# Linear-attention and gated-FFN kernel on one core: a third place for scores and P, other places for the 64-row blocks' k and v, and weight pairs that lie 1.5 pieces ahead of their words

## Chip, cores and metric

One core of one Trainium2 chip runs the whole program. The metric is the device time of one execution in microseconds: 651.5 us before the change, the median of three runs (650.5 to 652.1).

## What is computed

Attention with a memory over 4 batches, 8 heads, 576 tokens and 64 features per head, and then a gated FFN with an RMS norm over the 2304 tokens (model width 512, inner width 1536). Cut to what matters:

```python
scores = (q @ k.T) / sqrt(64);  scores[causal] = -1e9
a = exp(scores - max);  a = a / (a.sum(-1) + 1e-9);  local = a @ v
qp = where(q > 0, q + 1, exp(q))
mem = (qp @ M_prev) / (qp @ z_prev + 1e-6)
x = sigmoid(beta) * mem + (1 - sigmoid(beta)) * local
xn = x / sqrt(mean(x*x) + 1e-6) * rms_g
g = xn @ w_gate
out = (g * sigmoid(g) * (xn @ w_val)) @ w_out
```

w_gate, w_val, w_out and rms_g arrive as 64-bit words.

## The kernel before

**Tiling.** The tokens are cut into 18 blocks of 128 rows. Of each pair of batches eight blocks are full blocks of one batch, and the ninth holds the last 64 rows of both (the 64-row blocks are 8 and 17, and `is_tail` names them). Two blocks make one chunk of the FFN, so there are nine chunks of 256 tokens. The FFN of a chunk takes 12 tiles F of the inner width (`m_proj`: gate and val into PSUM tile gv), and the product with w_out (`m_down`: PSUM tiles out0 and out1).

**Attention of a block** goes in units, each a group of four heads or fewer: `u_scores` (scores on PE, L515, and masked into the SBUF tile S by DVE, L521, with the maximum nm), `u_exp` (exp on ACT in place, L567, and a cast of its f16 part into P16, L572), `u_lo` (the remainder S - P16 into the second half of P16, on DVE or POOL, L581, and then one DMA transpose of P16 into PT, L583), and `u_pv` (PV on PE, L605 to L607). In the names of the trace P16 is P. S and P16 take the pool's two places each. `mem` (L642) is phi(q) times the memory, from the transposed tile phT. When a block's t is summed, ACT takes its square sum xs (L244) and casts it to x (L95), and a DMA transpose gives xT, which a chunk's first product (L872) needs. Blocks 0 and 1 and chunk 0 are computed in f32 (L865, L919), everything later in f16 with three terms per product (L872; L927 to L929).

**Weights.** There are 24 pieces of w_gate and w_val in three thirds (eight pieces a third: two matrices, four slices of the model width), and 12 pieces of w_out. They are loaded as 64-bit words, turned to f32 (`f64_to_f32`, L781 to L783), and after a scale for the third is known (rgs, wos) split into a pair of f16 halves, in place: the pair p lies one slot ahead of its words, so that the hi half of p covers the first half of the words of p - 1, and the lo half the second. `split` has two ways:

```python
if way == "0":
    hi_cast(dst_hi, src, scale)          # ACT L95
    lo_cast(dst_lo, src, scale, dst_hi)  # DVE L98
...
nc.vector.tensor_scalar(src, src, scale, None, op0=ALU.mult)  # way 3: L112
nc.scalar.copy(dst_hi, src)                                   # L114
nc.gpsimd.tensor_tensor(dst_lo, src, dst_hi, ALU.subtract)    # L117
```

`SPLIT` is the table of ways by third; its third entry "033" sends five of the last third's eight pieces by way 3.

**Places.** `load_kv` brings a block's k and v into one of four places of the tag kv (4 KB per partition), or, for a 64-row block, into the one place of the tag kvt. The tag kT has ten places of 2 KB, the tag res has one place of 4 KB, through which the outputs leave (L905) and some words of w_out come (rawo).

**Order.** SyncE issues nearly all DMAs from one queue in program order. The order on each engine is set when the program is built: a list of attention steps with costs, and `run`, `zipped` and `proj` near L1175 to L1200, which lay weight splits and FFN tiles between them; a scheduler then moves instructions by priority and by when a place is free.

Of the kernel before, what the change touches and what calls it, by code (L numbers as in the profile page):

```python
# [9 lines left out]
F32 = mybir.dt.float32  # L10
# [32 lines left out]
SPLIT = ("0", "0", "033", "0")  # L43
# [15 lines left out]
def attn_memory_moe_kernel(  # L59
# [112 lines left out]
    wgv = const.tile([P, 2 * NC * NT3 + 1, 512], F32, name="wgv")  # L172
    wo = const.tile([P, NF + 1, 512], F32, name="wo")
    wgv16 = wgv.bitcast(F16)
    wo16 = wo.bitcast(F16)
# [28 lines left out]
    zs = const.tile([P, 4], F32, name="zs")  # L204

    def load_kv(n):
        tag = "kvt" if is_tail[n] else "kv"
        stage[n] = sb.tile([P, 2, HD], F32, tag=tag, name=f"kv{n}", bufs=1 if is_tail[n] else 4)
        if n >= 2:
            nc.sync.dma_start(out=stage[n], in_=qkv[n, :, :2, :])  # L210

    def load_half(n, j):
        nc.sync.dma_start(out=stage[n][:, j], in_=qkv[n, :, j, :])
# [37 lines left out]
    def stat_blk(b, i):  # L251
        if b < 2:
            r = slice(0, P) if i < NI else slice(b * TR, b * TR + TR)
            src = pre.pop((b, i), None)
            if src is None:
                kv = stage[blk_of[(b, i)] if i < NI else NI * 2]
                src = [kv[r, j] for j in range(2)]
            for j in range(2):
                if i == 0:
                    csum["kv", b, j] = ps.tile([P, 512], F32, tag="out", name=f"csum{j}")  # L260
                gram(csum["kv", b, j], src[j], i == 0, i == NI)
                if i == NI:
                    nc.vector.tensor_reduce(
                        stt[b][:, j, 0:1], csum.pop(("kv", b, j))[:, :P], axis=AX.X, op=ALU.max
                    )
            return
        if i < NI:
            for j in range(2):
                square_acc(stage[blk_of[(b, i)]][:, j], stt[b][:, j, i : i + 1])
        else:  # L270
            n = blk_of[(b - b % 2, NI)]
            r0 = (b % 2) * TR
            for j in range(2):
                square_acc(stage[n][r0 : r0 + TR, j], stt[b][r0 : r0 + TR, j, NI : NI + 1])
# [119 lines left out]
    def prep_qk32(n):  # L394
        k32[n] = sb.tile([P, NC, P], F32, tag="kT", name=f"k32_{n}", bufs=10)
        last["k", n] = transposed(k32[n], stage[n][:, 0], T32[0] == "a")
        q32[n] = sb.tile([P, 2, NC, P], F32, tag="qT", name=f"q32_{n}")
        last["q", n] = transposed(q32[n][:, 0], qst[n], T32[1] == "a")
# [163 lines left out]
    def u_exp(n, h0):  # L562
# [5 lines left out]
        p16 = sb.tile([P, 2 * (NI * P + P)], F16, tag="P16", name="P16")  # L568
# [442 lines left out]
    def lead_steps(n):  # L1011
# [18 lines left out]
        if n == NI * 2 - 1:  # L1030
            st[6].append((0.0, lambda: load_kv(blk_of[(nb, NI)])))
# [186 lines left out]
    run(zipped([lambda d=d: (m_down(d), wo_split(d)) for d in range(NF)], spl(2)), goal)  # L1218
# [79 lines left out]
```

## Time and profile before

| | before |
|---|---|
| runs | 651.5 us median, 650.5 to 652.1, three runs |
| profiled execution, its own time | 652.67 us |
| its span in the trace | 651.0 us |
| mean granted TensorE clock | 0.964 |
| PE (TensorE matmul) busy | 606.2 us, 93% |
| DVE busy | 468.1 us, 72% |
| ACT busy | 383.2 us, 59% |
| POOL busy | 172.7 us, 27% |

A timeline row gives an instruction's start and length, its engine, line, operation, what it writes and reads, the shape, and in brackets how long the engine was idle before it and what ended that. Positions in us count from the start of the span. PE matmuls overlap in the pipeline, so the length of one matmul row is longer than the distance to the next; a row with x20 is a run of twenty.

### The profile page before, as it was taken

Reading aid. Unit: us, or ns where it says so; the run is one execution under the profiler, and the core shown is the slowest. Engines: PE = TensorE matmul, PEld = TensorE weight load, DVE = VectorE, ACT = ScalarE, POOL = GpSimd, SP = SyncE. Lnnn points to the kernel's source line nnn. Section 1 sums busy time; section 2 is a strip of 40 time slices with the busy share of each in tenths; the row PEclk is TensorE's granted clock in tenths of the full one; section 3 lists DMA queues with packets and bytes.
Section 4 is the critical chain, followed back from the end, with each engine's and each line's share of the span. In section 5 each row is a group of like instructions: output and inputs, shape, how many; then the busy total and the mean of one; then the engine's idle time right before and its main releaser. Section 6 shows DMA issues by size and latency. Waiting matters only on the chain.

```text
span 651.0 us, 16007 instructions
## 1 busy us (share of the span) xinstructions
PE 606.2 (93%) x6131; PEld 472.7 (73%) x6131; DVE 468.1 (72%) x1444; ACT 383.2 (59%) x803; POOL 172.7 (27%) x257
## 2 busy tenths in 40 slices
PE   6899997898999599898999999999999999999996
PEld 4788785456766388687787777777878788888774
DVE  4689997788989765796877857968887757862221
ACT  4446776477688756575567666756665545532222
POOL 4020331112463333231242312422232212112211
PEclk9689998798999889999999999999999999999999
DMA  8977999539437997546859773595657464440001
GB/s 255 406 257 281 265 284 193 84 54 231 81 81 157 169 185 136 83 88 130 166 113 176 138 121 74 95 159 110 132 119 115 91 84 87 86 75 18 32 1 33
DMA packets 188524, 88.63 MB, mean 136 GB/s; under 512 B 173568, under 2 KB 173600, under 8 KB 188448
## 3 DMA queue, kind: packets, MB, share of 16 engines
q1 hardware_dynamic: 187680, 85.49, 61.0%
q0 software_dynamic: 768, 2.12, 1.0%
q8 instruction: 48, 0.79, 0.5%
q14 instruction: 28, 0.23, 0.1%
HBM read 36.20 MB, written 4.72 MB: 63 GB/s over the span
## 4 chain that ended last, share of the span: by engine, by line
PE 38%; DVE 7%; ACT 5%; DMA 5%; issue 3%; SPq 0%; POOL 0%; ACTq 0%
PE gv L872 20%; PE out L927 3%; PE out L928 3%; PE out L929 3%; PE sc L541 2%; DVE P L581 2%; PE sc L515 1%; DMA PT<-P 1%; DMA kT<-row 1%; ACT junk L244 1%; DMA xT<-x 1%; DVE S L521 1%; ACT S L567 1%; DVE th L883 1%; DMA kv<-in_qkv_dram 1%
## 5 line engine op out<-in xcount | busy, mean ns | idle before, releaser
L872 PE MATMUL gv<-xT,wgv 128*128 128x256 f16 x2304 | 314.0, 275 | 3.5 <-DMA xT<-x 3.5
L872 PEld LDWEIGHTS <-wgv 128*128 128x128 f16 x2304 | 221.9, 98 | 40.3 <-issue 4.4
L898 POOL TENSOR_TENSOR h<-th,h 128x256 f16<-128x256 f32 x96 | 71.5, 745 | 262.7 <-ACT h L897 204.8
L567 ACT ACTIVATE S<-S,nm 128x256 f32<-128x256 f32 (+4 forms) x128 | 75.2, 608 | 49.2 <-DVE nm L528 33.0
L515 PE MATMUL sc<-kT,qT 128*128 128x128 f16 x608 | 84.1, 220 | 3.1 <-DMA qT<-qT 1.4
L581 DVE TENSOR_TENSOR P<-S,P 128x512 f16<-128x512 f32 (+2 forms) x84 | 61.7, 735 | 26.0 <-ACT P L572 25.6
L883 DVE SCALAR_TENSOR_TENSOR th<-th,gv 128x256 f32<-128x256 f32 x96 | 39.9, 415 | 56.3 <-ACT th L882 55.7
L882 ACT ACTIVATE th<-gv,wt 128x256 f32<-128x256 f32 x96 | 44.7, 466 | 53.1 <-PE gv L872 52.1
L928 PE MATMUL out<-wo,h 128*128 128x512 f16 x192 | 72.8, 379 | 0.0
L927 PE MATMUL out<-wo,h 128*128 128x512 f16 x192 | 71.7, 379 | 0.0
L929 PE MATMUL out<-wo,h 128*128 128x512 f16 x192 | 71.7, 379 | 0.0
L521 DVE CUSTOM_DVE_ANT_0 S<-sc,mask,qsc 128x256 f32<-128x256 f32 (+3 forms) x112 | 62.0, 573 | 12.9 <-PE sc L515 7.3
L572 ACT CAST P<-S 128x512 f16<-128x512 f32 (+2 forms) x100 | 59.5, 595 | 10.8 <-DMA PT<-P 9.7
L897 ACT CAST h<-th 128x256 f16<-128x256 f32 x96 | 38.4, 400 | 46.1 <-DVE th L886 45.9
L605 PE MATMUL loc<-v,PT 128*128 128x65 f16 x304 | 50.0, 196 | 11.1 <-DMA PT<-P 11.1
L515 PEld LDWEIGHTS <-qT 128*128 128x128 f16 x608 | 50.9, 98 | 9.3 <-issue 3.1
L607 PE MATMUL loc<-v,PT 128*128 128x65 f16 x304 | 49.8, 195 | 0.0
L606 PE MATMUL loc<-v,PT 128*128 128x64 f16 x304 | 49.7, 196 | 0.0
L865 PE MATMUL gv<-xT,wgv 128*128 128x256 f32 x192 | 46.5, 395 | 2.1 <-DVE h32e L886 1.6
L886 DVE SCALAR_TENSOR_TENSOR th<-th,wt,gv 128x256 f32<-128x256 f32 x96 | 45.7, 477 | 1.7
L605 PEld LDWEIGHTS <-PT 128*128 128x128 f16 x304 | 29.5, 99 | 17.1 <-DMA PT<-P 13.9
L865 PEld LDWEIGHTS gv<-xT,wgv 128*128 128x128 f32 x192 | 36.4, 195 | 7.4 <-DVE h32e L886 1.8
(226 smaller groups left out, 1111.7 us busy)
## 6 DMA issues: line engine op xcount, KB each, us to landing
kv<-in_qkv_dram SPq DMA_DIRECT2D x16, 512.0 KB, 4.4
wo<-in_moe_w_gate_dram SPq DMA_DIRECT2D x12, 512.0 KB, 6.4
wo<-in_moe_w_val_dram SPq DMA_DIRECT2D x12, 512.0 KB, 5.5
q<-in_qkv_dram SPq DMA_DIRECT2D x18, 256.0 KB, 3.1
wo<-in_moe_w_out_dram SPq DMA_DIRECT2D x8, 512.0 KB, 5.5
qT<-qT SPq DMA_DIRECT2D x32, 128.0 KB, 2.6
out_dram<-res SPq DMA_DIRECT2D x16, 256.0 KB, 2.2
pre<-in_qkv_dram POOLq DMA_DIRECT2D x8, 256.0 KB, 7.1
```

The costliest lines, as they stand in the source:

```text
L515: nc.tensor.matmul(t[:, g * w + j * P : g * w + (j + 1) * P], qT[n][:, t2, h, :], kT[blk_of[(b, j)]][:, h, :], start=(t2 == 0), stop=(t2 = ...
L521: nc.vector.tensor_tensor_reduce(out=s[:, g * w : (g + 1) * w], in0=t[:, g * w : (g + 1) * w], in1=mask[:, m0 : m0 + w], scale=qsc[n][:, 5:6],
L567: nc.scalar.activation(v_, v_, AF.Exp, bias=nm[:, g : g + 1], scale=-1.0)
L572: nc.scalar.copy(p16[:, : G * w], s[:, : G * w])
L581: eng.tensor_tensor(p16[:, w : 2 * w], s[:, :w], p16[:, :w], ALU.subtract)
L605: nc.tensor.matmul(a, phi_, vhi, start=(j == 0), stop=False)
L865: nc.tensor.matmul(o, wgv[:, 1 + p, o0 : o0 + P], xT[0][:, cc, :], start=(cc == 0), stop=(cc == NC - 1))
L872: nc.tensor.matmul(o, lhs, xT[c][:, rhs, :], start=(cnt == 0), stop=(cnt == 3 * NC - 1))
L898: nc.gpsimd.tensor_tensor(h16[:, 1], th, h16[:, 0], ALU.subtract)
L927: nc.tensor.matmul(o, hh, whi, start=(f == 0), stop=False)
L928: nc.tensor.matmul(o, hh, wlo, start=False, stop=False)
L929: nc.tensor.matmul(o, hl, whi, start=False, stop=(f == NF - 1))
```

## The change

1. S and P16 get three places instead of two (`u_scores`, `u_exp`, `scores32`).
2. The tag kvt is gone. Block 8's k and v are loaded as two halves into two places of kT. Block 17's k and v are first loaded into the place of res (`load_tail`), only for their square sums, which are now two squares over 128 rows and two small POOL copies in place of four squares over 64 rows; and they are loaded a second time, into a place of kv, after block 13.
3. The words and pairs of all weights lie in one tile. A pair lies 1.5 slots ahead of its words: the hi half of p covers the second half of the words of p - 2, the lo half the first half of the words of p - 1. The first w_out pair's place now covers words of the last w_gate/w_val pieces.
4. All weight pieces are split by way 0.
5. In the order of the program, the splits of the last third all stand ahead of the splits of w_out; before, the two were interleaved.

```diff
-SPLIT = ("0", "0", "033", "0")
+SPLIT = ("0", "0", "0", "0")
...
-    wgv = const.tile([P, 2 * NC * NT3 + 1, 512], F32, name="wgv")
-    wo = const.tile([P, NF + 1, 512], F32, name="wo")
-    wgv16 = wgv.bitcast(F16)
-    wo16 = wo.bitcast(F16)
+    NW = 2 * NC * NT3
+    wall = const.tile([P, 256 + (NW + 1 + NF) * 512], F32, name="wgv")
+    wgv = wall[:, 256:].rearrange("p (s f) -> p s f", f=512)
+    wo = wgv[:, NW:, :]
+    wgv16 = wall.bitcast(F16)[:, : (NW + NF) * 1024].rearrange("p (s f) -> p s f", f=1024)
+    wo16 = wgv16[:, NW:, :]
...
     def load_kv(n):
-        tag = "kvt" if is_tail[n] else "kv"
-        stage[n] = sb.tile([P, 2, HD], F32, tag=tag, name=f"kv{n}", bufs=1 if is_tail[n] else 4)
+        if n == NI * 2:
+            stage[n] = [
+                sb.tile([P, H, P], F16, tag="kT", name=f"kv{n}_{j}", bufs=10)
+                .bitcast(F32).rearrange("p a b -> p (a b)") for j in range(2)
+            ]
+            for j in range(2):
+                load_half(n, j)
+            return
+        t = sb.tile([P, 2, HD], F32, tag="kv", name=f"kv{n}", bufs=4)
+        stage[n] = [t[:, j] for j in range(2)]
         if n >= 2:
-            nc.sync.dma_start(out=stage[n], in_=qkv[n, :, :2, :])
+            nc.sync.dma_start(out=t, in_=qkv[n, :, :2, :])
...
+    def load_tail(n):
+
+        t = sb.tile([P, 2, HD], F32, tag="res", name=f"tail{n}", bufs=1)
+        nc.sync.dma_start(out=t, in_=qkv[n, :, :2, :])
+        tail2["raw"] = t
...
-            n = blk_of[(b - b % 2, NI)]
-            r0 = (b % 2) * TR
-            for j in range(2):
-                square_acc(stage[n][r0 : r0 + TR, j], stt[b][r0 : r0 + TR, j, NI : NI + 1])
+            if "raw" in tail2:
+                t = tail2.pop("raw")
+                for j in range(2):
+                    square_acc(t[:, j], tail_ss[:, j : j + 1])
+            r = slice(b % 2 * TR, b % 2 * TR + TR)
+            nc.gpsimd.tensor_copy(stt[b][r, :2, NI], tail_ss[r])
...
-        s = sb.tile([P, NI * P + P], F32, tag="S", name="S")
+        s = sb.tile([P, NI * P + P], F32, tag="S", name="S", bufs=3)
...
-        p16 = sb.tile([P, 2 * (NI * P + P)], F16, tag="P16", name="P16")
+        p16 = sb.tile([P, 2 * (NI * P + P)], F16, tag="P16", name="P16", bufs=3)
...
         if not is_tail[n] and full.index(n) + NI < len(full):
             load_kv(full[full.index(n) + NI])
+        elif not is_tail[n] and full.index(n) + NI == len(full):
+            load_kv(NBLK - 1)
...
-            st[6].append((0.0, lambda: load_kv(blk_of[(nb, NI)])))
+            st[6].append((0.0, lambda: load_tail(blk_of[(nb, NI)])))
...
-    run(zipped([lambda d=d: (m_down(d), wo_split(d)) for d in range(NF)], spl(2)), goal)
+    run(zipped([lambda d=d: m_down(d) for d in range(NF)], spl(2) + [lambda d=d: wo_split(d) for d in range(NF)]), goal)
```

**How the order moves.** Up to about 88 us, apart from the place of block 8's loads, and in the last third of the program, the rows are the same. Three places follow, one on PE and two on ACT; in the changed kernel lines up to L204 keep about their numbers and later ones stand 19 to 21 lines lower (L515 is L536, L567 is L588, L572 is L593, L642 is L663, L872 is L893, L905 is L926, L244 is L263).

PE early in chunk 1's FFN in f16, before (about 149 to 153 us): gv_1612 is that chunk's second tile F, mem_0 is phi(q) times the memory for block 4 (phT is the transposed phi(q)); a LDWEIGHTS stands ahead of each MATMUL.

```order
L872 LDWEIGHTS wgv
L872 MATMUL gv_1612<-xT_1089,wgv 128x256
L872 LDWEIGHTS wgv
L872 MATMUL gv_1612<-xT_1089,wgv 128x256
L642 LDWEIGHTS phT_1587
L642 MATMUL mem_0_1690<-M_0_506,phT_1587 128x65
L642 LDWEIGHTS phT_1587
L642 MATMUL mem_0_1690<-M_0_506,phT_1587 128x65
```

The place of mem_0 after the change:

```order
L893 LDWEIGHTS wgv
L893 MATMUL gv_2002<-xT_1090,wgv 128x256
L893 LDWEIGHTS wgv
L893 MATMUL gv_2002<-xT_1090,wgv 128x256
L663 LDWEIGHTS phT_1588
L663 MATMUL mem_0_1691<-M_0_507,phT_1588 128x65
L663 LDWEIGHTS phT_1588
L663 MATMUL mem_0_1691<-M_0_507,phT_1588 128x65
```

gv_2002 is the chunk's fourth tile F. Before the change mem_0 stands behind the 48 matmuls of the chunk's first two tiles; now it stands behind 83 (24 of each of the first three tiles and 11 of the fourth).

ACT at the first splits of w_out, before (about 172 to 181 us): wo<-wo,wos is the hi half of a pair of w_out, wgv<-wgv,rgs and the CAST wgv<-wgv are pieces of the last third, S<-S,nm and P<-S are block 4's last units and block 5's first.

```order
L572 CAST P_1932<-S 128x384
L567 ACTIVATE S<-S,nm 128x384
L114 CAST wgv<-wgv 128x512
L572 CAST P_1979<-S 128x384
L95 ACTIVATE row_2270<-q_2103,qsc 128x8x64
L95 ACTIVATE wo<-wo,wos 128x512
L95 ACTIVATE wgv<-wgv,rgs 128x512
L567 ACTIVATE S<-S,nm 128x384
L572 CAST P_2086<-S 128x384
L95 ACTIVATE wo<-wo,wos 128x512
L114 CAST wgv<-wgv 128x512
```

The same place after the change (wgv<-wgv,wos is now the hi half of a pair of w_out):

```order
L95 ACTIVATE wgv<-wgv,rgs 128x512 x2
L588 ACTIVATE S<-S,nm 128x384
L593 CAST P_1976<-S 128x384
L95 ACTIVATE wgv<-wgv,rgs 128x512
L588 ACTIVATE S<-S,nm 128x384
L95 ACTIVATE wgv<-wgv,rgs 128x512
L593 CAST P_2082<-S 128x384
L95 ACTIVATE wgv<-wgv,wos 128x512
L588 ACTIVATE S<-S,nm 128x384
L593 CAST P_2129<-S 128x384
L95 ACTIVATE wgv<-wgv,wos 128x512
```

Before, the first w_out pair stands behind six casts of P of blocks 4 and 5, and five pieces of the last third stand behind it; now it stands behind seven casts, and behind all pieces of the last third.

ACT in block 6, at the end of chunk 1, before (about 212 to 222 us): x<-t,xs is what xT of chunk 2 is transposed from, res<-out are chunk 1's outputs.

```order
L567 ACTIVATE S<-S,nm 128x512
L572 CAST P_2813<-S 128x512
L567 ACTIVATE S<-S,nm 128x512
L905 ACTIVATE res<-out_0_2071,wos 128x512
L905 ACTIVATE res<-out_1_2072,wos 128x512
L572 CAST P_2927<-S 128x512
L244 ACTIVATE junk,xs<-t_5_2356 128x512
L356 ACTIVATE ph<-q_2611 128x512
L567 ACTIVATE S<-S,nm 128x512
L244 ACTIVATE junk,stt_2198<-kv_2656 128x512
L95 ACTIVATE x_2850<-t_5_2356,xs 128x512
```

The same place after the change:

```order
L588 ACTIVATE S<-S,nm 128x512
L593 CAST P_2809<-S 128x512
L903 ACTIVATE th<-gv_2792,wt 128x256
L263 ACTIVATE junk,xs<-t_5_2352 128x512
L377 ACTIVATE ph<-q_2607 128x512
L588 ACTIVATE S<-S,nm 128x512
L263 ACTIVATE junk,stt_2194<-kv_2652 128x512
L918 CAST h_2850<-th 128x256
L95 ACTIVATE x_2846<-t_5_2352,xs 128x512
L95 ACTIVATE row_2947<-kv_997,cb_663 128x8x64
L593 CAST P_2923<-S 128x512
```

The two res rows no longer stand here (they stand five rows further on), and x stands ahead of the second cast of P in this place instead of behind it.

## Rows read from the trace of the kernel before

**Rows 1.** The page: busy time of each engine with its share and instructions.

```profile
PE 606.2 (93%) x6131; PEld 472.7 (73%) x6131; DVE 468.1 (72%) x1444; ACT 383.2 (59%) x803; POOL 172.7 (27%) x257
```

**Rows 2.** Busy time in four stretches; columns in the first row, PEclk is the granted clock.

```profile
core 0: us, PE busy (x) PEld busy (x) DVE busy (x) ACT busy (x) POOL busy (x), PEclk, DMA share, GB/s
90.00:120.00 30.00, 23.03 (x256) 18.96 (x255) 24.24 (x88) 18.70 (x38) 4.99 (x6) 0.87 0.96 196
120.00:165.00 45.00, 41.77 (x259) 25.22 (x258) 36.27 (x125) 29.92 (x60) 8.10 (x12) 0.93 0.61 126
165.00:232.00 67.00, 55.13 (x606) 41.30 (x603) 56.21 (x172) 52.35 (x107) 29.26 (x34) 0.92 0.66 127
232.00:651.00 419.00, 407.31 (x4496) 322.05 (x4494) 281.04 (x830) 231.26 (x484) 106.43 (x155) 1.00 0.54 101
```

**Rows 3.** Timeline of PE, 104 to 118 us: start, length, instruction, idle before and releaser.

```profile
104.67 0.20 PE L605 MATMUL loc<-v,PT 128*128 128x65 f16 x1 [1.88 <-DMA PT<-P]
117.61 0.59 PE L134 MATMUL allp<-ident,wmx 128*2 128x128 f32 x2 [1.33 <-DVE nm L521]
```

**Rows 4.** Waits: engine, line, releaser: us in total, times, longest.

```profile
ACT P L572 <- DMA PT<-P: 9.7, 10, 2.2
ACT wgv L95 <- DVE wgv L98: 6.2, 7, 1.5
ACT row L95 <- DMA xT<-x: 13.0, 9, 3.1
```

**Rows 5.** Timeline of PE, 145 to 177 us.

```profile
145.39 2.67 PE L872 MATMUL gv<-xT,wgv 128*128 128x256 f16 x23
152.34 0.66 PE L642 MATMUL mem<-M,phT 128*128 128x65 f16 x16 [3.03 <-DMA phT<-row]
152.84 4.00 PE L872 MATMUL gv<-xT,wgv 128*128 128x256 f16 x20
176.21 0.59 PE L927 MATMUL out<-wo,h 128*128 128x512 f16 x2
```

**Rows 6.** Timeline of PE, 219 to 233 us.

```profile
219.08 0.20 PE L605 MATMUL loc<-v,PT 128*128 128x65 f16 x1 [2.15 <-DMA PT<-P]
221.39 0.20 PE L605 MATMUL loc<-v,PT 128*128 128x65 f16 x1 [1.33 <-DMA PT<-P]
224.08 0.24 PE L605 MATMUL loc<-v,PT 128*128 128x65 f16 x1 [1.13 <-DMA PT<-P]
228.41 4.54 PE L872 MATMUL gv<-xT,wgv 128*128 128x256 f16 x25 [3.48 <-DMA xT<-x]
```

**Rows 7.** Timelines of ACT and DVE, 216 to 219 us.

```profile
216.35 0.62 ACT L572 CAST P<-S 128x512 f16<-128x512 f32 x1 [2.23 <-DMA PT<-P]
218.29 0.75 DVE L521 CUSTOM_DVE_ANT_0 S<-sc,mask,qsc 128x512 f32<-128x512 f32 x1 [2.53 <-POOL P L581]
```

**Rows 8.** Groups of one shape: busy us, mean ns of one, idle before and releaser.

```profile
L98 DVE SCALAR_TENSOR_TENSOR wgv<-wgv,rgs 128x512 f16<-128x512 f32 x19 | 15.2, 799 | 3.9 <-ACT wgv L95 3.9
L112 DVE TENSOR_SCALAR wgv<-wgv,rgs 128x512 f32<-128x512 f32 x5 | 3.2, 689 | 0.0
L95 ACT ACTIVATE wgv<-wgv,rgs 128x512 f16<-128x512 f32 x19 | 13.6, 715 | 8.4 <-DVE wgv L98 6.2 <-DVE rgs L809 2.2
L114 ACT CAST wgv<-wgv 128x512 f16<-128x512 f32 x5 | 3.0, 610 | 0.6 <-DVE wgv L98 0.6
L117 POOL TENSOR_TENSOR wgv<-wgv 128x512 f16<-128x512 f32 x5 | 5.9, 1172 | 9.7 <-ACT wgv L114 9.7
```

**Rows 9.** The page, DMA issues: count, KB each, median us from issue to landing.

```profile
kv<-in_qkv_dram SPq DMA_DIRECT2D x16, 512.0 KB, 4.4
```

**Rows 10.** Timelines of DVE and POOL, 176 to 179 us.

```profile
176.58 0.74 DVE L98 SCALAR_TENSOR_TENSOR wo<-wo,wos 128x512 f16<-128x512 f32 x1
177.24 1.40 DVE L98 SCALAR_TENSOR_TENSOR wgv<-wgv,rgs 128x512 f16<-128x512 f32 x1
177.07 1.02 POOL L581 TENSOR_TENSOR P<-S,P 128x384 f16<-128x384 f32 x1 [1.50 <-ACT P L572]
```

More of the change, by code (lines that the diff above doesn't have):

```diff
@@ L203, in attn_memory_moe_kernel @@
     zhl = const.tile([P, 2, B * H], F16, name="zhl")
-    zs = const.tile([P, 4], F32, name="zs")
+    zs = const.tile([P, 6], F32, name="zs")
+    tail_ss = zs[:, 4:6]
     def load_kv(n):
-        tag = "kvt" if is_tail[n] else "kv"
-        stage[n] = sb.tile([P, 2, HD], F32, tag=tag, name=f"kv{n}", bufs=1 if is_tail[n] else 4)
+        if n == NI * 2:
[8 more added lines that the diff above has]
+        stage[n] = [t[:, j] for j in range(2)]
         if n >= 2:
-            nc.sync.dma_start(out=stage[n], in_=qkv[n, :, :2, :])
+            nc.sync.dma_start(out=t, in_=qkv[n, :, :2, :])
     def load_half(n, j):
-        nc.sync.dma_start(out=stage[n][:, j], in_=qkv[n, :, j, :])
+        nc.sync.dma_start(out=stage[n][j], in_=qkv[n, :, j, :])
+    tail2 = {}
+    def load_tail(n):
+        t = sb.tile([P, 2, HD], F32, tag="res", name=f"tail{n}", bufs=1)
+        nc.sync.dma_start(out=t, in_=qkv[n, :, :2, :])
+        tail2["raw"] = t
     def load_M(b):
@@ L256, in stat_blk @@
                 kv = stage[blk_of[(b, i)] if i < NI else NI * 2]
-                src = [kv[r, j] for j in range(2)]
+                src = [kv[j][r] for j in range(2)]
             for j in range(2):
@@ L268, in stat_blk @@
             for j in range(2):
-                square_acc(stage[blk_of[(b, i)]][:, j], stt[b][:, j, i : i + 1])
+                square_acc(stage[blk_of[(b, i)]][j], stt[b][:, j, i : i + 1])
         else:
-            n = blk_of[(b - b % 2, NI)]
-            r0 = (b % 2) * TR
-            for j in range(2):
-                square_acc(stage[n][r0 : r0 + TR, j], stt[b][r0 : r0 + TR, j, NI : NI + 1])
+            if "raw" in tail2:
[4 more added lines that the diff above has]
+            nc.gpsimd.tensor_copy(stt[b][r, :2, NI], tail_ss[r])
     def stat_M(b):
@@ L395, in prep_qk32 @@
         k32[n] = sb.tile([P, NC, P], F32, tag="kT", name=f"k32_{n}", bufs=10)
-        last["k", n] = transposed(k32[n], stage[n][:, 0], T32[0] == "a")
+        last["k", n] = transposed(k32[n], stage[n][0], T32[0] == "a")
         q32[n] = sb.tile([P, 2, NC, P], F32, tag="qT", name=f"q32_{n}")
@@ L404, in prep_k @@
         c = consts_of(n)
-        t = split_rows(stage[n][:, 0], c[:, 0:1], RWAY[2])
+        t = split_rows(stage[n][0], c[:, 0:1], RWAY[2])
         kT[n] = sb.tile([P, H, P], F16, tag="kT", name=f"kT{n}", bufs=10)
@@ L410, in prep_v @@
         c = consts_of(n)
-        src = stage.pop(n)[:, 1].rearrange("p (h d) -> p h d", h=H)
+        src = stage.pop(n)[1].rearrange("p (h d) -> p h d", h=H)
         t = sb.tile([P, H, VW], F16, tag="v16", name=f"v16_{n}", bufs=10)
@@ L425, in scores32 @@
         t = [ps.tile([P, 4, P], F32, tag="sc", name="sc") for _ in range(2)]
-        Ssb[n] = [sb.tile([P, NI * P + P], F32, tag=tag, name="S") for tag in ("S", "P16")]
+        Ssb[n] = [sb.tile([P, NI * P + P], F32, tag=tag, name="S", bufs=3) for tag in ("S", "P16")]
         nm = tiny.tile([P, 2, 4], F32, tag="qsc", name="nm32", bufs=5)
@@ L468, in pv32 @@
                 nc.tensor.matmul(
-                    loc[:, 4 * u + g], pt[:, g, :], stage[n][:, 1, h * D : h * D + D],
+                    loc[:, 4 * u + g], pt[:, g, :], stage[n][1][:, h * D : h * D + D],
                     start=True, stop=True,
```

## The prediction, made before the changed kernel was timed

> **What bounds the kernel now.** I read the page first: PE is busy 93% of the span and no other engine over 72% [rows 1], so time can only come from PE's idle time, from its clock, or from work that PE does not do. Then the busy time by stretches [rows 2]. From 232 us to the end PE is busy 407.3 of 419.0 us at a granted clock of 1.00: nothing that the change moves there is waited for long. Before that it looks otherwise: PE stands idle 30.0 - 23.0 = 7.0 us between 90 and 120 us, 45.0 - 41.8 = 3.2 us between 120 and 165, and 67.0 - 55.1 = 11.9 us between 165 and 232, at a granted clock of 0.87, 0.93 and 0.92. That is about 22 us, and all that this change can save by removing waits lies in it. DVE is the next fullest engine there, 56.2 of 67 us in the last of the three. Then I read PE's timeline for what ended each idle stretch, and the waits for which of those a missing place can cause.
>
> **Third place for S and P.** ACT's cast into P waits for the DMA that reads the place's former content, ten times, 9.7 us in all [rows 4]. On PE the places show at three spots.
>
> *90 to 120 us.* PE waits 1.88 us for a PT, and 1.33 us behind a scores unit of block 3 [rows 3]. A third place lets the cast of the next unit start before the last transpose has been read, so I take the first, -1.9 us. The second ends on DVE's own order of work, which the change leaves; I count it as nothing. Bounds: 0 and -3.2 us (both).
>
> *165 to 232 us.* In block 6, ACT waits 2.23 us for a place of P, and DVE 2.53 us for a place of S that POOL still reads [rows 7]. The first wait runs from 214.12 to 216.35, the second from 215.76 to 218.29, so together they cover 4.17 us. Behind them PE waits 2.15, 1.33 and 1.13 us for PTs of block 6, and then 3.48 us for the xT of chunk 2 [rows 6], whose x stands on ACT behind these casts. The four are 8.1 us. If the two waits go, the chain to PT and xT gets up to 4.17 us shorter; what PE waits beyond that is the chain's own length (exp, cast, subtraction, transpose), which stays. I take -4.2 us, because it is the length of the removed waits themselves; in the new order x also stands ahead of one more cast, which helps that xT. Bounds: 0 and -8.1 us. What is late next there: the transpose itself, and SP's queue.
>
> **Pairs 1.5 pieces ahead.** Before, the hi half of pair p lay on words that DVE still had to read for the lo half of p - 1, and ACT waited seven times for it, 6.2 us in all, 1.5 at most [rows 4]. Now it lies on words of p - 2, which DVE has left one piece sooner, and the cast runs on. The wait itself is worth nothing directly: while the second third is split, PE works on chunk 0's output. Its worth is ACT's and DVE's time: the splits of the first two thirds are done earlier, and the chunk's tiles come forward. Before, PE stood 3.03 us for phT of block 4 [rows 5]; in the new order 35 more tile matmuls (83 instead of 48) stand ahead of that product. One takes 2.67 / 23 = 0.116 us at the high clock and 4.00 / 20 = 0.20 us at the low one [rows 5], so 35 of them are 4.1 to 7.0 us, more than the wait. I take -3.0 us. Bounds: 0 (the tiles' own th on ACT are late, or phT is late by as much) and -3.0 us.
>
> **All splits by way 0.** Five pieces of the last third change: DVE's 0.689 us become 0.799, ACT's 0.610 become 0.715, and POOL's 1.172 us go [rows 8]. That is +0.55 us on DVE, +0.53 us on ACT, -5.9 us on POOL. DVE is the fullest engine of that stretch beside PE [rows 2], so I count its 0.55 in full, as +0.6 us, ACT's beside it as nothing, and POOL's as nothing (it is busy 29 of 67 us). Bounds: 0 and +1.1 us.
>
> **64-row blocks.** Block 8's halves go into places of kT that nothing else wants so early. Block 17's extra load is 512 KB, 4.4 us from issue to landing [rows 9], after 232 us, where DMA is busy 54%; one instruction more on SP's queue. The statistics save two squares on ACT and cost two small copies on POOL. All of it lies beside PE's stream; I count 0. If SP's queue were the limit there, a transpose behind it would be late by the issue, under 1 us; upper bound +1.
>
> **Sum.** -1.9 - 4.2 - 3.0 + 0.6 = -8.5 us. The durations come from the profiled execution of 652.7 us, which gives 644.2; the median of the runs stands 1.2 us under it, so the forecast is **643.0 us**. Bounds of the terms alone: 3.2 + 8.1 + 3.0 = 14.3 us less and 2.1 us more, 637 to 653.6 against the median.
>
> **Rivals.**
>
> *No gain.* The third place is there, but what feeds the units is late as well. ACT waits 13.0 us in nine stretches for the xT transpose, before it casts a row [rows 4]: the two places for rows and SP's single queue are untouched, and a unit that could start earlier would then wait for its kT or qT. For it: nine waits of up to 3.1 us. Against it: they end on other rows than the waits in block 6. Then only the split's cost and a part of one stall are left, about 651 us.
>
> *Slower: w_out's pairs come too late.* In the new order every piece of the last third is split ahead of the first pair of w_out. Before, PE's first f16 product with w_out started at 176.21 us [rows 5], right behind that pair's hi cast, and five pieces of the last third stood behind the pair. Those five now go first: 5 x 0.80 = 4.0 us of DVE's time [rows 8], and one more unit of attention stands ahead, about 3 us by the distance of PE's products. PE has 14 more tile matmuls ahead of that product in its new order, 14 x 0.116 = 1.6 us. So PE would stand up to 4.0 + 3.0 - 1.6 = 5.4 us at the first w_out pair, everything behind it in PE's order (block 5's PV among it) waits too, and whatever was saved before 165 us is waited away there. With the 0.6 of the splits and nothing saved, 651.5 + 6.0 = 657.5; with the saving of block 6 kept, 653.3; I put it at 656 us. It decides from the point where the pair's hi cast ends after PE has reached the product. Against it: the pieces were split with waits before, and now run on; and the splits start earlier.
>
> *Faster: POOL's subtractions slowed DVE.* At 177.24 a DVE split took 1.40 us, while POOL's subtraction ran from 177.07 to 178.09; the same operation just before it took 0.74 [rows 10]. If the five removed POOL subtractions each cost DVE 0.66 us, 3.3 us of DVE's time come back in its fullest stretch: 643.0 - 3.3 = 639.7 us. Against it: DVE is not always at such an operation while POOL subtracts, and the mean of the splits is 0.80, near the undisturbed 0.74. The Trainium skill, page "SBUF — State Buffer", section "Who interferes with whom", says that a DVE instruction with two SBUF inputs and a GpSimd instruction that reads SBUF exclude each other for the whole instruction; by that rule the pieces' new way is a gain and no cost, and the pair of rows agrees with it.
>
> *Faster: the clock.* If PE, with fewer pauses, keeps the high clock in the three early stretches, its busy time there shrinks by 13% of 23.0, 7% of 41.8 and 8% of 55.1, 10.3 us; half of it on the path gives about 638 us. Against it: the longest pauses before 90 us are untouched.
>
> **How the numbers follow.** A measurement of this kernel can tell about 0.3%, 2 us, from no change, so "same" is 649.5 to 653.5. Forecast 0.52, no gain 0.14, w_out late 0.16, POOL 0.08, clock 0.10. Faster is the forecast, POOL and clock together: 0.70; same 0.14; slower 0.16. The range goes from 635 (a good part of the clock's case in) to 656 (the price that I gave the slower case); beyond lie about 0.1 on the slow side and some hundredths on the fast side.
>
> **What would show it.** Right: ACT's wait of the cast into P for PT under 3 us in total, no wait of the weight's hi cast for DVE, PE's idle time between 90 and 232 us down from 22 to about 14 us, and no stall at block 4's memory product. Wrong: PE waits at the first products with w_out (L948) for ACT or DVE; or the stall before chunk 2's first tile is as long as before; or PE's stream after 232 us, now 407 us busy of 419, has new gaps at the 64-row blocks or at block 13.

## The result and the profile after

The changed kernel took **641.5 us** (median of four runs, 638.8 to 642.5) against 651.0 us before in the same comparison (four runs, 647.8 to 652.1): a ratio of 0.9855 with a 95% interval of 0.9808 to 0.9903, so 1 to 2% faster. The forecast was 643.0 us. In the experiments below the kernel before ran many more times, at a median of 652.2 to 652.8 us.

The profiled execution of the changed kernel was its fastest (638.8 us), the one of before (652.7) was slower than the four timed here, so the two traces lie 13.9 us apart in span, more than the 9.5 us of the medians. The head of the page after:

```profile
span 637.1 us, 16046 instructions
PE 600.0 (94%) x6131; PEld 470.0 (74%) x6131; DVE 467.0 (73%) x1444; ACT 380.0 (60%) x799; POOL 168.4 (26%) x254
```

The same 6131 matmuls kept PE busy 6.2 us less than before [rows 1], and PE's idle time fell from 44.8 to 37.1 us. The first goes with the clock (0.964 to 0.981 in the mean), the second is the waits. How far two executions of one kernel differ can be seen from e5 below, whose trace has the instructions of before in the same order: PE is busy 603.7 us there, and chunk 2 begins 4.2 us sooner than in the trace of before. The stretches of [rows 2] again, with the same columns:

```profile
90.00:120.00 30.00, 24.94 (x233) 19.29 (x231) 28.10 (x115) 20.61 (x42) 5.24 (x6) 0.94 0.96 201
120.00:165.00 45.00, 42.29 (x357) 29.56 (x356) 38.70 (x121) 33.14 (x65) 10.71 (x14) 1.00 0.54 118
165.00:232.00 67.00, 57.78 (x676) 43.33 (x674) 56.89 (x163) 51.98 (x106) 24.78 (x31) 0.97 0.80 149
232.00:637.00 405.00, 395.67 (x4342) 312.08 (x4339) 271.19 (x813) 222.56 (x468) 103.70 (x153) 1.00 0.55 101
```

Idle time of PE between 90 and 232 us fell from 22.1 to 17.0 us, and the granted clock rose in each of the three stretches (0.87 to 0.94, 0.93 to 1.00, 0.92 to 0.97). In e5's trace of the order of before the idle time is 20.0 us, so some 2 of the 5 us lie between two executions. After 232 us PE is as full as before.

The waits that answer to [rows 4], and the one wait of PE for an xT that is left (it stands before chunk 1, at 137.94 us):

```profile
ACT row L95 <- DMA xT<-x: 11.1, 9, 2.4
ACT P L593 <- DMA PT<-P: 5.1, 3, 3.7
ACT wgv L95 <- DVE wgv L98: 3.2, 6, 0.9
PE gv L893 <- DMA xT<-x: 0.7, 1, 0.7
```

ACT's wait for a place of P fell from 9.7 us in ten to 5.1 in three, of which 0.4 us, at 211.32, stands ahead of chunk 2's first matmul; the hi cast's wait for DVE fell from 6.2 to 3.2. On PE's timeline these rows answer to [rows 3, 5, 6]:

```profile
105.06 0.20 PE L626 MATMUL loc<-v,PT 128*128 128x65 f16 x1 [0.71 <-DMA PT<-P]
109.65 0.20 PE L626 MATMUL loc<-v,PT 128*128 128x65 f16 x1 [2.31 <-DMA PT<-P]
148.29 0.41 PE L663 MATMUL mem<-M,phT 128*128 128x65 f16 x8
171.07 0.60 PE L948 MATMUL out<-wgv,h 128*128 128x512 f16 x2
211.29 0.20 PE L626 MATMUL loc<-v,PT 128*128 128x65 f16 x1 [2.04 <-DMA PT<-P]
212.64 0.20 PE L626 MATMUL loc<-v,PT 128*128 128x65 f16 x1 [0.53 <-DMA PT<-P]
214.79 0.20 PE L626 MATMUL loc<-v,PT 128*128 128x65 f16 x1 [0.56 <-DMA PT<-P]
216.36 3.55 PE L893 MATMUL gv<-xT,wgv 128*128 128x256 f16 x31
```

Four things are to be seen. The PT waits of the units at 105 and 110 us are still there (3.0 us in place of 1.88). What went in that stretch are two waits for DVE, of a small transpose and of a memory product, which stand in before at

```profile
113.31 0.38 PE L134 MATMUL allp<-ident,wmx 128*2 128x128 f32 x2 [1.05 <-DVE fl L673]
114.36 0.42 PE L642 MATMUL mem<-M,phT 128*128 128x65 f16 x8 [0.67 <-DVE t L676]
```

The first of them is in the trace of every kernel with two places of S (1.1 to 1.6 us) and in none with three. The wait at 117.61 in [rows 3] is gone too, but e5's trace of the order of before has none there either. Block 4's memory product at 148.29 waits for nothing. Block 6's PTs are still waited for, 2.04 + 0.53 + 0.56 = 3.1 us in place of 4.6. And the run of 31 that begins at 216.36, chunk 2's first 24 matmuls and 7 of the next tile, waits for nothing: before, chunk 2 began at 228.41 after 3.48 us [rows 6]. Two rows of ACT tell why:

```profile
170.03 0.72 ACT L95 ACTIVATE wgv<-wgv,wos 128x512 f16<-128x512 f32 x1 [0.28 <-DVE wgv L98]
209.59 0.72 ACT L95 ACTIVATE x<-t,xs 128x512 f16<-128x512 f32 x1
```

The first pair of w_out has its hi cast at 170.03, in time for PE's product at 171.07, and the x of block 5, from which chunk 2's xT is made, is cast at 209.59; before they were at 174.56 and 222.00:

```profile
174.56 0.72 ACT L95 ACTIVATE wo<-wo,wos 128x512 f16<-128x512 f32 x1 [0.25 <-DVE wos L829]
222.00 0.71 ACT L95 ACTIVATE x<-t,xs 128x512 f16<-128x512 f32 x1
```

From chunk 2's first matmul to the end it is 637.1 - 216.4 = 420.7 us after and 651.0 - 228.4 = 422.6 before. So of the 13.9 us between the traces 12.0 are won before that point.

### The profile page after: what moved, and what is told of

It reads as the page before. It is cut to its first block, busy times and chain, and to the rows that moved or that the text cites. A ratio compares the mean times of both kernels' runs of the same rounds, so it can differ in the third digit from the quotient of the medians.

```text
span 637.1 us, 16046 instructions
## 1 busy us (share of the span) xinstructions
PE 600.0 (94%) x6131; PEld 470.0 (74%) x6131; DVE 467.0 (73%) x1444; ACT 380.0 (60%) x799; POOL 168.4 (26%) x254
## 4 chain that ended last, share of the span: by engine, by line
PE 59%; DMA 17%; DVE 12%; issue 5%; ACT 5%; SPq 1%; POOL 1%; ACTq 0%; POOLq 0%; DVEq 0%
PE gv L893 28%; PE out L950 5%; PE out L949 5%; PE out L948 5%; DMA PT<-P 4%; PE sc L536 3%; DMA wgv<-in_moe_w_out_dram 2%; PE gv L886 2%; DMA kv<-in_qkv_dram 2%; PE sc L562 2%; DMA wgv<-in_moe_w_val_dram 2%; DMA qT<-row 2%; DVE wgv L98 2%; PE out L940 2%; DVE S L542 1%
## 5 line engine op out<-in xcount | busy, mean ns | idle before, releaser
L893 PE MATMUL gv<-xT,wgv 128*128 128x256 f16 x2304 | 310.1, 273 | 2.7 <-DVE th L907 1.9
L893 PEld LDWEIGHTS <-wgv 128*128 128x128 f16 x2304 | 220.2, 98 | 36.8 <-issue 3.8
L588 ACT ACTIVATE S<-S,nm 128x256 f32<-128x256 f32 (+4 forms) x128 | 74.7, 607 | 48.1 <-DVE nm L549 35.9
L536 PE MATMUL sc<-kT,qT 128*128 128x128 f16 x608 | 82.6, 220 | 2.1 <-DMA qT<-qT 1.4
L948 PE MATMUL out<-wgv,h 128*128 128x512 f16 x192 | 72.0, 380 | 1.3 <-ACT res L926 1.3
L949 PE MATMUL out<-wgv,h 128*128 128x512 f16 x192 | 73.3, 382 | 0.0
L950 PE MATMUL out<-wgv,h 128*128 128x512 f16 x192 | 72.5, 382 | 0.0
L593 ACT CAST P<-S 128x512 f16<-128x512 f32 (+2 forms) x100 | 59.2, 595 | 6.2 <-DMA PT<-P 5.1
L626 PE MATMUL loc<-v,PT 128*128 128x65 f16 x304 | 48.5, 194 | 12.0 <-DMA PT<-P 11.9
L536 PEld LDWEIGHTS <-qT 128*128 128x128 f16 x608 | 50.5, 98 | 7.9 <-DMA qT<-qT 1.7
L628 PE MATMUL loc<-v,PT 128*128 128x65 f16 x304 | 48.3, 193 | 0.0
L627 PE MATMUL loc<-v,PT 128*128 128x64 f16 x304 | 48.0, 194 | 0.0
L886 PE MATMUL gv<-xT,wgv 128*128 128x256 f32 x192 | 44.3, 384 | 2.1 <-DVE h32e L907 1.6
```

The lines of the kernel that those rows point to most:

```text
L536: nc.tensor.matmul(t[:, g * w + j * P : g * w + (j + 1) * P], qT[n][:, t2, h, :], kT[blk_of[(b, j)]][:, h, :], start=(t2 == 0), stop=(t2 = ...
L588: nc.scalar.activation(v_, v_, AF.Exp, bias=nm[:, g : g + 1], scale=-1.0)
L593: nc.scalar.copy(p16[:, : G * w], s[:, : G * w])
L626: nc.tensor.matmul(a, phi_, vhi, start=(j == 0), stop=False)
L886: nc.tensor.matmul(o, wgv[:, 1 + p, o0 : o0 + P], xT[0][:, cc, :], start=(cc == 0), stop=(cc == NC - 1))
L893: nc.tensor.matmul(o, lhs, xT[c][:, rhs, :], start=(cnt == 0), stop=(cnt == 3 * NC - 1))
```

## The experiments

The theory that came out of the prediction: the third place and the pairs' new distance each save waits before 232 us, the way of splitting costs next to nothing, the rest is free. Rivals: the clock does it; POOL's removed subtractions do it; one of the two parts does it alone. Ratios are to the kernel before on the same chip.

| run | edit | us | ratio, 95% interval |
|---|---|---|---|
| e1 | changed, two places for S and P16 | 656.5 | 1.0052 (1.0030 to 1.0074) |
| e2 | changed, way 3 back | 640.6 | 0.9804 (0.9777 to 0.9831) |
| e3 | changed, pairs one slot ahead | 645.4 | 0.9874 (0.9845 to 0.9904) |
| e4 | before, PE's stalls in block 6 filled | 652.8 | 0.9992 (0.9967 to 1.0017) |
| e5 | before, w_out's splits last in the program (the instructions' order stayed) | 651.8 | 0.9988 (0.9968 to 1.0008) |
| e6 | before, the 64-row blocks' places | 651.6 | 0.9995 (0.9970 to 1.0020) |
| e7 | changed, S two, P16 three | 653.2 | 1.0004 (0.9989 to 1.0020) |
| e8 | changed, S three, P16 two | 657.8 | 1.0091 (1.0070 to 1.0113) |
| e9 | before, all by way 0 | 652.5 | 0.9994 (0.9965 to 1.0024) |
| e10 | changed, two places, way 3 back | 656.3 | 1.0043 (1.0013 to 1.0073) |
| e11 | changed, HLAG = 3 | 641.0 | 0.9818 (0.9778 to 0.9858) |
| e12 | changed, NPM = 1 | 643.1 | 0.9851 (0.9815 to 0.9887) |

### The third place: e1, e7, e8

```diff
 e1
-        s = sb.tile([P, NI * P + P], F32, tag="S", name="S", bufs=3)
+        s = sb.tile([P, NI * P + P], F32, tag="S", name="S")
-        p16 = sb.tile([P, 2 * (NI * P + P)], F16, tag="P16", name="P16", bufs=3)
+        p16 = sb.tile([P, 2 * (NI * P + P)], F16, tag="P16", name="P16")
```

The places that `scores32` takes go with them (not shown). e7 makes the first of the two edits alone, e8 the second alone.

> The changed kernel with two places for S and P16, all else as changed. Theory 'places and pairs' (the prediction's): the 6.1 us of the third place come back, about 647.6 us, ACT's cast into P waits again some 10 us for PT, and PE waits again in block 6 and before chunk 2. Rival 'pairs alone' (the earlier splits bring all, the third place stands unused): 641.5 us, within 1. Rival 'clock': as the first theory in time, but a good part of the difference is PE's busy time, with the granted clock under 0.9 in some stretch between 105 and 232 us where the changed kernel has 1.00.

> The changed kernel with two places for S and three for P16. Theory 'P decides' (P16 is held until its DMA transpose has read it, S only until the subtraction): within 3 us of the changed kernel, 641 to 644. Rival 'a unit needs both places': as with two of each, 653 to 657. Rival 'half and half': 648 to 650.

> The changed kernel with three places for S and two for P16. Theory 'P decides': 652 to 656, ACT's cast into P waits about 10 us for PT as before the change. Rival 'a unit needs both': the same here, so the pair with the run before tells. Rival 'S decides': 641 to 644.

Without the third places nothing of the gain is left: e1 is slower than before, 9 us above the 647.6 of the prediction's theory, and no theory on record had that. With one of them nothing is left against before either, so "a unit needs both" holds, and "P decides" is out. P16's third place alone is worth something against e1 all the same: 1.0004 against 1.0052, intervals that don't meet, some 3 us of the 15 that both bring. The view of waits of e1 has ACT's cast where it was before the change:

```profile
ACT P L593 <- DMA PT<-P: 12.0, 9, 2.4
```

e7 and e8, the same view, each with the cast's wait for a place of P, DVE's wait for the scores, and PE's wait before a chunk. e7, P16 three and S two:

```profile
ACT P L593 <- DMA PT<-P: 1.9, 2, 1.3
DVE S L542 <- PE sc L536: 11.2, 14, 1.8
PE gv L893 <- DMA xT<-x: 5.2, 1, 5.2
```

e8, S three and P16 two:

```profile
ACT P L593 <- DMA PT<-P: 19.9, 17, 2.6
DVE S L542 <- PE sc L536: 4.4, 8, 1.4
PE gv L893 <- DMA xT<-x: 9.2, 2, 7.0
```

In e8 the missing place is plain to see: 19.9 us of the cast. (The 7.0 us of PE stand before chunk 1 there, the other 2.2 before chunk 2.) In e7 that wait has nearly gone (1.9 us), and yet the time is that of before. The reason is the order: all 6131 matmuls of e7 stand in the order of e1, although P16 has three places, so the order was laid for two places of S; 224 scores matmuls in f16 stand ahead of chunk 2's first, as before the change, where the changed kernel has 230. The missing place of S shows as an order, not as a wait for it. DVE's wait for the scores (11.2 us, 7.3 before) can't tell this: e2, which is fast, has 15.5. PE's timeline of e1 shows what follows, at the first matmul of chunk 2:

```profile
232.13 4.21 PE L893 MATMUL gv<-xT,wgv 128*128 128x256 f16 x19 [5.06 <-DMA xT<-x]
```

### The clock: e4

```diff
             a = accs[n, g4][:, hh, :]
+            if n == 6 and 1 <= h <= 4:
+                w0 = v16[blk_of[(b, 0)]].rearrange("p h e -> p (h e)")
+                for _ in range(24 if h < 4 else 60):
+                    nc.tensor.matmul(a, w0[:, :P], w0[:, : D + 1], start=True, stop=True)
             for j in range(nb):
```

> The kernel before with 132 matmuls of 65 columns added on PE, 24 ahead of the PV of heads 1, 2 and 3 of block 6 and 60 ahead of head 4's, that is where PE waited between 219 and 228 us; they write what the next product overwrites, and by the spacing of PV matmuls (about 0.03 us) are 4 us of PE work. Theory 'waits alone' (the clock gives nothing): no change or up to 1 us slower, 651 to 652 us, since what PE waits for comes no sooner. Theory 'clock': the granted clock from 215 to 232 us rises from 0.70 to 0.9 or more, the first matmuls of chunk 2 run at the high clock (24 in 2.8 us instead of 4.4), and the kernel gets 1.5 to 2.7 us faster, about 649 us.

The time did not move, as "waits alone" said, though the clock from 215 to 232 us rose to the 0.90 that "clock" asked for. Busy time in the stretch, with the columns of [rows 2], and then PE's first row of chunk 2:

```profile
215.00:225.00 10.00, 6.29 (x183) 5.95 (x180) 6.95 (x19) 8.23 (x18) 3.34 (x5) 1.00 1.12 203
215.00:232.00 17.00, 11.80 (x222) 10.28 (x219) 10.38 (x33) 11.83 (x25) 5.22 (x7) 0.90 1.02 186
225.00:235.00 10.00, 8.51 (x75) 7.08 (x75) 6.14 (x21) 5.25 (x10) 2.55 (x3) 0.83 0.90 184
```

```profile
226.49 4.56 PE L876 MATMUL gv<-xT,wgv 128*128 128x256 f16 x25 [2.23 <-DMA xT<-x]
```

The filled stretch to 225 us kept a clock of 1.00 (0.83 before), so the pauses do bring the clock down. But the added matmuls did not reach the last pause: PE still stood 2.23 us for xT, the clock fell behind it, and 25 matmuls took 4.56 us as in [rows 6] (4.54). So filling the pauses among the PTs is worth nothing that can be measured, while the clock at chunk 2's start was not raised by this run. What the fall behind the xT wait costs can be read from rows: e2 has 25 of the same matmuls, after a wait of 2.00 us but at a clock of 1.00, in 2.90 us, so about 1.6 us. That the clock rises goes with the removed waits, and is part of their worth: the profiles of the kernels that gained (after, e2, e3, e11, e12) have PE busy 598.5 to 601.8 us, those that did not (before, e1, e5 to e10) 603.7 to 607.8, for the same 6131 matmuls.

### The pairs: e3 and e10

```diff
 e3
-    wall = const.tile([P, 256 + (NW + 1 + NF) * 512], F32, name="wgv")
-    wgv = wall[:, 256:].rearrange("p (s f) -> p s f", f=512)
+    wall = const.tile([P, (NW + 1 + NF) * 512], F32, name="wgv")
+    wgv = wall.rearrange("p (s f) -> p s f", f=512)
```

e10 is e1 with the edit of e2.

> The changed kernel with pairs one slot ahead of their words, as before the change, in the joint tile. Theory 'places and pairs': 3.0 us slower, 644.5 us, ACT's hi cast waits again some 6 us in all for DVE's lo half. Rival 'places alone': 641.5 us, within 1. Rival 'pairs alone': about 650 us.

> The changed kernel with two places for S and P16 and with way 3 back for five pieces, so pairs, order and 64-row blocks are as changed. Theory 'the way costs where S and P16 have two places': 652, as before the change. Rival 'the pairs cost there': 656, as with two places and way 0.

With three places and pairs one slot ahead the kernel takes 645.4 us, near the 644.5 of "places and pairs". On the same chip in the same comparison e2 took 640.6, and the intervals don't meet; e2 differs from e3 in the way of splitting too, which e9 shows to be worth nothing in the kernel before. The direct comparison of e3 with the changed kernel goes across two sessions, and there the intervals overlap (0.9874 and 0.9855). So the shift is worth some 1 to 5 us, the prediction's 3.0 among them. But it does not work where the prediction had it. Waits of e3 (the trace is of its fastest run, 642.5 us):

```profile
ACT wgv L95 <- DVE wgv L98: 10.3, 10, 2.3
PE out L948 <- ACT wgv L95: 2.3, 2, 1.9
```

ACT's hi casts of the first two pairs of w_out, and PE's products that need them:

```profile
181.78 0.71 ACT L95 ACTIVATE wgv<-wgv,wos 128x512 f16<-128x512 f32 x1
186.26 0.72 ACT L95 ACTIVATE wgv<-wgv,wos 128x512 f16<-128x512 f32 x1
```

```profile
182.54 0.59 PE L948 MATMUL out<-wgv,h 128*128 128x512 f16 x2 [0.46 <-ACT wgv L95]
187.03 0.59 PE L948 MATMUL out<-wgv,h 128*128 128x512 f16 x2 [1.85 <-ACT wgv L95]
```

In e3 block 4's memory product waits 0.31 us (3.03 before), so its stall went without the shift; and block 5's x is cast at 207.54, sooner than in the changed kernel. What is late are w_out's pairs: first cast at 181.78 instead of 170.03, the last at 219.66 instead of 192.74, and chunk 1's output leaves PSUM at 230.69 instead of 216.78. PE waits 2.3 us for the hi half, as the prediction's slower rival said. Only a part of this is the wait for DVE: of the 10.3 us six waits with 5.2 us belong to the splits before the last third, as before the change, and two with 3.6 us to w_out's. The larger part is order: on ACT w_out's first cast stands behind 21 casts of P in e3, the last behind 30; in the changed kernel they stand behind 15 and 22. Why the distance of the pairs moves the order so far is not shown. Chunk 2 begins with no wait, 2.6 us later than in the changed kernel, and the rest takes 421.8 us:

```profile
218.94 0.27 PE L893 MATMUL gv<-xT,wgv 128*128 128x256 f16 x1
```

With two places the same shift gives nothing. e10 has pairs, order and the 64-row blocks' places as changed, and is 0.4% slower than before, the 656 us of "the pairs cost there". Its first row of chunk 2:

```profile
231.66 4.66 PE L893 MATMUL gv<-xT,wgv 128*128 128x256 f16 x21 [5.42 <-DMA xT<-x]
```

Chunk 2 begins at 231.66, 3.3 us later than before, and the rest takes 424.6 us, 2.0 longer than before. The places of the 64-row blocks cost nothing by themselves (e6), nor does the way of splitting (e9). What is left are the pairs in their joint tile and the order of the splits, which no run has apart. In e10 w_out's twelve hi casts stand behind 15 to 20 casts of P on ACT, in before behind 14 to 23, so they are crowded into fewer units of attention; whether that is what makes the attention late stays open.

### The rest of the change by itself: e5, e6, e9

```diff
 e5
-    run(zipped([lambda d=d: (m_down(d), wo_split(d)) for d in range(NF)], spl(2)), goal)
+    run(zipped([lambda d=d: m_down(d) for d in range(NF)], spl(2) + [lambda d=d: wo_split(d) for d in range(NF)]), goal)
 e9
-SPLIT = ("0", "0", "033", "0")
+SPLIT = ("0", "0", "0", "0")
```

e6 is the kernel before with `load_kv`, `load_tail`, `load_next` and the statistics of the 64-row blocks as in the change.

> The kernel before with one line of the change: all splits of the last third stand ahead of w_out's in the program's order. With two places the rest of the change made the kernel 0.5% slower than before, and something in it must cost. Theory 'order costs' (the slower rival of the prediction): 2 to 6 us slower, 654 to 658, PE waits at the first f16 product with w_out for ACT's hi cast. Rival 'the order is free': 652, within 1, and the cost is in the 64-row blocks or in the pairs.

> The kernel before with only the change of the 64-row blocks' places (no kvt, block 17 loaded twice, block 8 in two places of kT), and two places for S and P16. The prediction counted it as nothing: 652, within 1. Rival 'the loads cost': 2 to 5 us slower, with PE's busy share after 232 us lower than before (407 of 419).

> The kernel before with all pieces of the last third split by way 0, nothing else. With two places for S and P16 the rest of the change made the kernel 4 us slower, and neither the order nor the 64-row blocks do so alone; this run and the next look for which part does. Theory 'the way costs where S and P16 have two places': about 656, 4 us slower. Rival 'the pairs cost there': 652 here, within 1.5. The prediction's own price for the way is +0.6 us; theory 'POOL's subtractions slow DVE' gives 3.3 us less, 649.

All three are the kernel before within 0.4%. But e5 says nothing of the order: in its trace the instructions stand on every engine as in before, so the line alone moves none of them. ACT's first casts of w_out in e5:

```profile
171.51 0.72 ACT L95 ACTIVATE wo<-wo,wos 128x512 f16<-128x512 f32 x1 [0.94 <-DVE wos L829]
172.14 0.70 ACT L95 ACTIVATE wgv<-wgv,rgs 128x512 f16<-128x512 f32 x1
173.90 0.72 ACT L95 ACTIVATE wo<-wo,wos 128x512 f16<-128x512 f32 x1
174.56 0.62 ACT L114 CAST wgv<-wgv 128x512 f16<-128x512 f32 x1
```

Five pieces of the last third still stand behind w_out's first, as before the change. All pieces stand ahead of it in the nine kernels that have both the line and the joint tile, where the first w_out pair lies on words of the last pieces, and in none of the other five. So "the order is free" is not shown: no run has the new order alone. What e5 gives is a second trace of the order of before. Block 17's second load and block 8's places are as free as the prediction counted them; what they give is room, 4 KB per partition of the 5 KB that the third places take (the rest comes from the half slot that the joint tile saves).

### POOL's subtractions: e2 and e12

```diff
 e2
-SPLIT = ("0", "0", "0", "0")
+SPLIT = ("0", "0", "033", "0")
 e12
-NPM = 2
+NPM = 1
```

> The changed kernel with five pieces of the last third split by way 3 again. Theory of the prediction (the way's durations add up on DVE): 0.6 us faster, 640.9 us, not to be told from no change. Rival 'POOL's subtractions slow DVE': 3.3 us slower, 644.8 us, and DVE's operations that overlap one of the five subtractions take about 1.4 us instead of 0.74. No theory expects over 646.

> The changed kernel with NPM = 1: all subtractions S - P16 of blocks 4 to 7 on POOL, not every second one. That takes 16 subtractions of 0.57 to 0.76 us off DVE before 232 us and puts them on POOL at 1.15 us. Theory 'DVE's load is on the path': 2 to 5 us faster, 637 to 639. Rival 'the length of a unit's chain is on the path' (subtraction and transpose follow one another): 0.4 to 0.6 us more per unit, 2 to 6 us slower, and PE waits longer for PT in blocks 4 to 6. Rival 'POOL's subtractions slow DVE': slower, with DVE's operations of two inputs up from 0.75 us.

With five POOL subtractions back, e2 is no slower than the changed kernel. Its groups that answer to [rows 8]:

```profile
L98 DVE SCALAR_TENSOR_TENSOR wgv<-wgv,rgs 128x512 f16<-128x512 f32 x19 | 15.3, 803 | 0.8
L117 POOL TENSOR_TENSOR wgv<-wgv 128x512 f16<-128x512 f32 x5 | 6.6, 1323 | 7.5 <-DVE wgv L98 6.4 <-ACT wgv L114 1.0
```

DVE's splits by way 0 take 0.803 us (0.793 in the changed kernel), POOL's subtractions 1.32 us (1.17 before). None of these splits ran during one of the five subtractions, so their mean doesn't tell what those cost, and the rival's 1.4 us was not put to the test on them. Two small DVE operations did meet one: 128x2 at L365 took 0.72 us and 128x3 at L850 took 1.05, each until that subtraction's end, against 0.14 and 0.22 in the changed kernel. The first of them and its subtraction:

```profile
162.82 1.15 POOL L117 TENSOR_TENSOR wgv<-wgv 128x512 f16<-128x512 f32 x1 [1.03 <-ACT wgv L114]
163.27 0.72 DVE L365 TENSOR_TENSOR qsc<-qsc,cb 128x2 f32<-128x2 f32 x1
```

The two make 1.4 us more of DVE's time, and the kernel's time shows none of it. By the rule of the Trainium skill, page "SBUF — State Buffer", section "Who interferes with whom", a DVE instruction with two SBUF inputs and a GpSimd instruction that reads SBUF contend for an exclusive lock; the trace agrees at the row of 0.72 us, which has two such inputs, and the time of e2 shows that it decides nothing here.

e12 puts every subtraction of blocks 4 to 7 on POOL. Its groups of 128x512:

```profile
L602 POOL TENSOR_TENSOR P<-S,P 128x512 f16<-128x512 f32 x16 | 18.4, 1158 | 20.0 <-ACT P L593 15.9 <-PE loc L628 3.0 <-PE gv L893 1.2
L602 DVE TENSOR_TENSOR P<-S,P 128x512 f16<-128x512 f32 x36 | 26.3, 729 | 16.2 <-ACT P L593 16.0
```

On POOL one takes 1.16 us, on DVE 0.73. PE's waits for PTs of block 6 grew:

```profile
213.53 0.20 PE L626 MATMUL loc<-v,PT 128*128 128x65 f16 x1 [3.19 <-DMA PT<-P]
221.58 0.20 PE L626 MATMUL loc<-v,PT 128*128 128x65 f16 x1 [3.81 <-DMA PT<-P]
```

3.19 and 3.81 us, where the changed kernel has 2.04, 0.53 and 0.56. The x of block 5 is cast at 214.71 instead of 209.59, so a unit's own chain is on the path there. The time went from 641.5 to 643.1, inside the intervals: neither the gain that "DVE's load is on the path" had at 2 to 5 us nor a loss that can be told from none.

### A unit more in flight: e11

```diff
-HLAG = 2
+HLAG = 3
```

> The changed kernel with HLAG = 3: PV of blocks 2 and 3 follows its scores by three units instead of two, as in all other blocks. In the changed kernel PE still waits 0.71 and 2.31 us at 105 and 110 us for a PT of these blocks. Theory 'the third place allows a third unit in flight': these two waits go and x of blocks 2 to 5 comes 2 to 3 us earlier, 638 to 639 us. Rival 'the wait only moves': 641, within 1.5, with the same wait on the next product or before chunk 1's first tile.

PE's waits between 100 and 115 us in e11:

```profile
106.67 0.20 PE L626 MATMUL loc<-v,PT 128*128 128x65 f16 x1 [0.59 <-DMA PT<-P]
107.72 0.20 PE L626 MATMUL loc<-v,PT 128*128 128x65 f16 x1 [0.66 <-DMA PT<-P]
112.11 0.20 PE L626 MATMUL loc<-v,PT 128*128 128x65 f16 x1 [1.81 <-DMA PT<-P]
```

3.1 us at three rows in place of 3.0 at two, and 641.0 us: the wait only moved, as the rival said. No run here beats the changed kernel by more than the interval.

## Why the prediction was right, and where not

The number, the sign and the range were right. Point by point:

- **What bounds the kernel.** That only PE's idle time and clock before 232 us can be won was right, and sharper than put: in all the traces, 14 kernels, chunk 2 begins between 216.1 and 232.1 us, and the rest takes 420.0 to 425.0 us. To within those 5 us the date of chunk 2's first matmul is the kernel's time.
- **Third place, 165 to 232 us: -4.2 us.** Right in place, too small. Block 4's x is cast 6.6 us sooner than before (189.43 against 195.98), block 5's 12.4 sooner: 5.9 us are won between the two. Against e5's trace of the order of before it is 2.8 and 8.6, and again 5.8 between the two. The wait for xT went as a whole in this trace (in e2, as fast, 2.00 us of it stay), the one for PTs by a third, so the step "what PE waits beyond that is the chain's own length, which stays" held for the PTs and failed for xT. With the pairs one slot ahead the places are worth about 652.2 - 645.4 = 6.8 us, near the 6.1 of the two terms of the places; with the pairs as changed 656.5 - 641.5 = 15, across sessions.
- **Third place, 90 to 120 us: -1.9 us.** About right in size, by the wrong rows. PE's idle time in this stretch is 4.2 to 5.7 us in the six kernels with three places of S and 5.5 to 8.3 in the eight with two, some 2 us less in the mean. But the PT wait that the term named is still there, and what went are waits for DVE that the term did not name. Block 2's x came 2.8 us sooner than in the trace of before and 0.5 sooner than in e5's, so its date doesn't show the gain.
- **Pairs: -3.0 us.** The size fits (1 to 5), the step failed. Block 4's memory product waits 3.0 to 3.2 us in before, e4, e5, e6 and e9, where it stands behind two tiles of chunk 1, and 0.3 us at most in every kernel whose order sets it later: in the changed one, but also in e1, e7, e8 and e10, which gained nothing. So that stall was filled as the term said and was worth nothing by itself. In before, e1, e7, e8 and e10 PE then stands 2.2 to 5.4 us for the xT of chunk 2, made from block 5's x; that sets the date. What goes with the pairs when there are three places is that w_out's splits come in time (e3), by their order more than by the wait for DVE.
- **Way 0: +0.6 us.** Not to be told from nothing, both ways round (e2, e9).
- **64-row blocks: 0.** Right (e6).
- **Sum.** It added terms that are not independent. With two places the pairs, with the order that comes with them, cost some 3 us (e10), with three they save 1 to 5; without the pairs the places save about 7. That the sum came out is in part luck: it counted too much idle time (22.1 us between 90 and 232 fell to 17.0, not to 14), one term named a stall that was worth nothing, and the clock, which stands among the rivals and not in the sum, comes with 6.2 us less busy time between the two traces (3.7 against e5's).
- **Signs.** Of the four that it set for being right one came as written, no stall at block 4's memory product. ACT's cast waits 5.1 us for PT, not under 3; the hi cast's wait for DVE was halved and not gone; and the idle time stayed above 14 us. None of the signs of being wrong came: PE waits for no w_out pair, starts chunk 2 without a wait, and is busy 395.7 of 405.0 us after 232.
- **Rivals.** "No gain" fell. "w_out late" did not come in the changed kernel, whose first pair had its hi cast 4.5 us sooner than before though more splits stand ahead of it, but it is there in e3 (2.3 us at L948), and in e1, e7 and e11 with 1.1 to 1.5 us. "POOL" fell as a price (e2). "The clock" was not a rival but a part: it goes with the waits, and filling pauses without ending the last wait gives nothing (e4).

## What to carry to other kernels

A place more for one tile of a chain can be worth little or nothing while the next tile of the same chain still has too few: test the places together, and look for a missing place in the order of the instructions too, since a program that is laid out for two places shows no wait for the third. Compare the order of the instructions before taking an edit for a test: e5's edit moved no row, and its time says nothing of the order. Where one engine is full from some date to the end, that date is the time of the kernel: measure every edit by it. And a stall on the full engine is worth its length only if the work that it delays is what that date waits for; price edits that share a stretch together, since what one of them frees, another may need.

## What the runs showed of the hardware

After pauses of 1.1 to 3.5 us between products (before) and of 2.23 us (e4) PE ran its next 25 matmuls of 128x256 in 4.54 and 4.56 us, and where the clock had stayed up, after a pause of 2.00 us (e2), in 2.90 us; added matmuls in the pauses held the granted clock at 1.00 for as long as they lasted (215 to 225 us in e4), and it fell again behind the first pause without them. The profiles of the kernels that gained have PE's busy time for the same matmuls 2 to 9 us shorter than those that did not.
